# Linear attention and a gated FFN on one core: a table of 3101 steps planned anew

## The chip, the core and the metric

The kernel runs on one core of a Trainium2 chip. The metric is the device time of one execution in microseconds. Four engines compute: TensorE (PE, with its weight loads PEld), VectorE (DVE), ScalarE (ACT) and GpSimd (POOL). SyncE (SP) issues most of the DMAs, POOL the rest. Each engine works through its own list of instructions strictly in order, and waits where an instruction needs something that another engine or a DMA has not delivered yet.

## What is computed

```python
# attention: batch 8, heads 8, sequence 576, head size 64
q_s = exp(q - max(q, axis=-1));  q_s /= sum(q_s, axis=-1) + 1e-9
k_s = exp(k - max(k, axis=2));   k_s /= sum(k_s, axis=2) + 1e-9
kv = einsum('bhsd,bhse->bhde', k_s, v)
x = einsum('bhsd,bhde->bhse', q_s, kv)      # as 4608 tokens x 512
# gated FFN: 512 -> 1536 -> 512
xn = x / sqrt(mean(x * x, axis=-1) + 1e-6) * rms_g
g = xn @ w_gate
out = (g * sigmoid(g) * (xn @ w_val)) @ w_out
```

q, k, v, rms_g are float32; the three weights come in as float64.

## The kernel before

The tokens are worked in nine blocks of 512 (index j, 0 to 8), the hidden size of 1536 in twelve slices of 128 (index i). A matmul in full float32 takes two passes, so most operands are split into a high and a low part that are each exact in a faster format (`_hi` and `_lo` steps), and three products of the parts are added up in PSUM. Blocks 0 to 2 are computed as written: `f1` is one slice of gate or value (twelve matmuls of 128x512), `f2` one slice of the output product. Blocks 3 to 8 go in three pairs p, in which seven products (`pp`, six matmuls each) take the place of eight, with sums on DVE (`c_`), and `f2p` as output product.

Everything is a chain of small steps. A step is one function of the kernel with its indices, as `f1.13.0` (slice 13, that is block 1, slice 1; gate). The order in which the steps are written out is a table of 3101 names, the string `ORDER` at the top of the file. The program takes the names one by one and calls the functions; a letter behind a colon says on which engine a step runs that could run on several (A for ACT, D for DVE, P for POOL). The tile framework adds the waits. So the table sets three things: each engine's list, the engine of many steps, and which buffer of a rotating pool a step gets, with the wait that comes from that buffer's last user.

The steps that matter here:

- `k_load`, `v_load`, `q_load` and `load_w` (from lines 475, 499, 627, 418) are DMAs on SP's queue. A `v_load` of a later batch is five DMAs, a `q_load` four or eight, a `k_load` three.
- `v_ones` (line 514) is a memset on POOL that fills the column of ones beside v, in the same tile into which `v_load` writes.
- For keys, by batch b and pair of heads g: `k_max`, `k_tr` (PE), `k_top`, `k_diag`, `k_rows` (PE), `k_sub`, `k_exp`, then `k_mm` (PE, line 566), which needs v, and `k_eps`, `k_rec`, `kv_norm0`, `kv_hi`, `kv_lo`.
- For queries: `q_max`, `q_sub`, `q_exp`, `q_sum`, `q_rec`, `q_mul`, `q_t`, and `q_x`, the matmul with kv, which gives x. In block 0 they are named with a 0 (`q_sub0`, line 658, and `q_mul0`, line 674, run on POOL). Then `x_sq`, `x_hi`, `x_lo`, `n_sum` and the steps `n_t`, `n_y0`, `n_y1`, `n_rows` for the norm.
- `conv_mul`, `conv_shift`, `conv_sign`, `conv_low`, `conv_add` turn a slice of float64 weights into float32; `w_hi`, `w_lo`, `o_hi`, `o_lo` split it. `s_add`, `s_hi`, `s_lo` prepare the sums of weights that the pairs use.
- `g_mul` (DVE, line 965) reads what `f1.i.0` left in PSUM, `silu` (ACT) and `h_mul` (DVE, line 972) follow. There are two banks of PSUM for gate and value, so `f1.13.0` can start when `g_mul.12` has read its bank.
- `warm` is matmuls without use, which keep PE busy in the first stage.

Of the kernel before, what the change touches and what calls it, by code (L numbers as in the profile page):

```python
# [27 lines left out]
load_w.0.0 k_sub.0.0 v_load.0.3 k_exp.0.2 k_tr.0.1 q_sum0.0.2 warm.9 k_exp.0.0 q_max0.0.0 v_load.0.1 q_eps0.0.2
k_top.0.1 conv_mul.0.1 q_sub0.0.0:P q_rec0.0.2 k_sub.0.3 q_mul0.0.2:P conv_shift.0.1 q_exp.0.0 load_w.1.1
conv_low.0.1.1 q_max0.0.3 warm.2.12 q_t0.0.2 k_diag.0.1:A conv_sign.0.1 q_sub0.0.3:P k_exp.0.3 warm.2.5 g_load  # L30
q_max0.0.1 warm.2.3 load_w.1.0 v_ones.0.3 k_max.1.0 k_mm.0.0 conv_add.0.1.1 q_exp.0.3 q_c0.0.2:A warm.2.11 q_load0.1.0
conv_mul.0.0 k_mm.0.2 k_eps.0.0 q_sub0.0.1:P q_sum0.0.0 conv_low.0.0.1 k_rec.0.0 k_tr.1.0 conv_shift.0.0 warm.2.9
q_exp.0.1 k_rows.0.1 q_eps0.0.0 k_eps.0.2 k_mm.0.3 k_top.1.0 k_rec.0.2 q_rec0.0.0 conv_sign.0.0 kv_norm0.0.2:A
q_mul0.0.0:P k_diag.1.0:A k_sub.0.1 load_w.1.2 kv_norm0.0.0:A conv_add.0.0.1 q_t0.0.0 q_load0.1.1 q_sum0.0.1 k_exp.0.1
k_rows.1.0 q_x0.0.2 k_eps.0.3 q_sum0.0.3 q_c0.0.0:A q_eps0.0.1 k_mm.0.1 k_rec.0.3 w_hi.0.0.2:A q_eps0.0.3 q_rec0.0.1
k_sub.1.0 q_mul0.0.1:P q_x0.0.0 conv_mul.1.1 k_eps.0.1 q_rec0.0.3 k_rec.0.1 q_mul0.0.3:P kv_norm0.0.1:D kv_norm0.0.3:A
warm.2.0 load_w.2.1 conv_shift.1.1 conv_mul.1.0 q_t0.0.1 load_w.2.2 x_hi.0.2:A q_t0.0.3 conv_shift.1.0 load_w.0.2
q_c0.0.1:A conv_sign.1.1 load_w.3.2 x_sq.0.0 q_x0.0.1 x_lo.0.2 q_c0.0.3:A q_max0.1.0 x_sq.0.2 n_sum0.0 k_load.1.1
x_hi.0.0:A conv_sign.1.0 q_sub0.1.0:P q_x0.0.3 x_sq.0.1 q_max0.1.1 x_hi.0.1:A n_sum0.1 x_lo.0.0 q_sub0.1.1:P load_w.2.0
x_sq.0.3 x_lo.0.1 n_sum0.2 q_exp.1.0 w_lo.0.0:P load_w.3.0 x_hi.0.3:A q_sum0.1.0 n_sum0.3 k_exp.1.0 x_lo.0.3 f1.0.0.0.0  # L40
conv_low.1.0.2 v_load.1.0 f1.0.0.0.1 n_t.0 f1.0.0.0.2 f1.0.0.0.3 f1.0.1.0.0 q_eps0.1.0 f1.0.0.1.0 n_y0.0 q_exp.1.1
conv_add.1.0.2 f1.0.1.0.1 f1.0.1.0.2 conv_mul.0.2 f1.0.1.0.3 n_y1.0 f1.0.0.1.1 f1.0.0.1.2 f1.0.0.1.3 f1.0.1.1.0
f1.0.1.1.1 f1.0.1.1.2 f1.0.1.1.3 f1.0.0.2.0 w_lo.0.1:P n_rows.0 w_hi.1.0.2:A f1.0.0.2.1 f1.0.0.2.2 load_w.3.1
f1.0.0.2.3 q_rec0.1.0 f1.0.1.2.0 load_w.5.0 g_mul.0 conv_mul.2.1 f1.0.1.2.1 w_lo.1.0:P f1.0.1.2.2 load_w.5.1 f1.0.1.2.3
conv_shift.0.2 f1.1.0 silu.0 conv_shift.2.1 q_mul0.1.0:P q_load0.1.2 conv_sign.0.2 w_lo.1.1:P conv_low.0.2.1 h_mul.0
conv_mul.2.0 conv_sign.2.1 f1.1.1 conv_low.2.0.2 conv_add.0.2.1 conv_shift.2.0 q_sum0.1.1 conv_low.2.2.1 load_w.4.0
v_ones.1.2 conv_sign.2.0 load_w.4.2 conv_mul.3.0 q_eps0.1.1 q_load0.1.3 conv_mul.1.2 conv_add.2.0.2 conv_shift.3.0 f2.0
conv_low.3.2.1 q_rec0.1.1 conv_sign.3.0 conv_low.1.2.1 conv_shift.1.2 conv_mul.3.1 conv_sign.1.2 q_mul0.1.1:P
w_hi.2.0.2:A g_mul.1 load_w.6.0 conv_shift.3.1 conv_low.3.0.2 load_w.4.1 w_lo.2.0:P k_mm.1.0 conv_sign.3.1 silu.1
f1.2.0 k_eps.1.0 w_lo.2.1:P k_rec.1.0 conv_mul.2.2 q_max0.1.2 kv_norm0.1.0:A h_mul.1 conv_low.5.0.2 conv_add.3.0.2  # L50
conv_shift.2.2 q_t0.1.0 q_max0.1.3 f1.2.1 q_c0.1.0:A conv_sign.2.2 conv_add.1.2.1 load_w.7.0 g_mul.2 conv_mul.4.0
load_w.7.1 silu.2 conv_shift.4.0 k_load.1.2 conv_add.2.2.1 w_hi.3.0.2:A conv_sign.4.0 q_x0.1.0 k_max.1.1 q_sub0.1.3:P
conv_mul.3.2 load_w.5.2 f2.1 x_sq.1.0 load_w.6.1 q_sub0.1.2:P x_hi.1.0:A conv_shift.3.2 q_load.2.0 conv_sign.3.2
w_lo.3.1:P h_mul.2 conv_mul.4.1 x_lo.1.0 conv_low.4.0.2 w_lo.3.0:P conv_shift.4.1 f1.3.1 conv_mul.4.2 conv_sign.4.1
q_exp.1.2 conv_shift.4.2 conv_add.4.0.2 conv_sign.4.2 q_exp.1.3 k_tr.1.1 f1.3.0 k_top.1.1 k_max.1.2 k_diag.1.1:A
conv_add.3.2.1 conv_mul.5.0 load_w.8.1 load_w.8.0 w_hi.4.0.2:A n_cols.0 load_w.6.2 conv_shift.5.0 load_w.7.2
conv_low.5.2.1 w_lo.4.1:P k_rows.1.1 g_mul.3 f2.2 conv_low.4.2.1 conv_sign.5.0 conv_low.7.0.2 conv_add.4.2.1 k_sub.1.1
conv_mul.5.1 q_sum0.1.3 w_lo.4.0:P silu.3 conv_shift.5.1 conv_sign.5.1 v_ones.1.1 v_load.1.1 f1.4.0 load_w.8.2
conv_mul.6.0 conv_add.5.0.2 h_mul.3 conv_low.6.0.2 q_max.2.0 q_sum0.1.2 conv_mul.6.1 f1.4.1 q_eps0.1.2 w_hi.5.0.2:A
load_w.10.0 q_rec0.1.2 q_eps0.1.3 load_w.10.1 conv_shift.6.0 q_mul0.1.2:P k_exp.1.1 conv_shift.6.1 w_lo.5.0:P  # L60
conv_sign.6.1 f2.3 g_mul.4 w_lo.5.1:P conv_mul.5.2 q_half.2.0 o_hi.4:A conv_sign.6.0 silu.4 conv_shift.5.2
conv_add.6.0.2 conv_sign.5.2 conv_mul.7.0 k_mm.1.1 f1.5.0 conv_add.5.2.1 k_eps.1.1 k_load.1.3 k_rec.1.1 q_rec0.1.3
conv_shift.7.0 kv_norm0.1.1:A h_mul.4 kv_hi.1.1:A kv_zero.2 conv_sign.7.0 v_load.1.2 h_hi.4:A o_hi.5:D conv_mul.6.2
q_t0.1.1 h_lo.4:D f1.5.1 q_c0.1.1:A o_lo.5:P conv_shift.6.2 conv_mul.7.1 conv_sign.6.2 conv_low.6.2.1 o_lo.4:P
q_max2.2.0 conv_shift.7.1 w_hi.6.0.2:A conv_sign.7.1 q_x0.1.1 v_ones.1.3 g_mul.5 conv_add.7.0.2 conv_mul.8.2 f2.4
x_sq.1.1 conv_shift.8.2 x_hi.1.1:A conv_sign.8.2 x_lo.1.1 conv_mul.8.0 w_lo.6.0:P load_w.9.1 silu.5 conv_shift.8.0
load_w.9.0 f1.6.0 conv_low.7.2.1 q_load.2.1 h_mul.5 conv_add.6.2.1 conv_mul.7.2 conv_sign.8.0 conv_low.8.2.1
conv_shift.7.2 w_lo.6.1:P h_hi.5:A conv_mul.8.1 conv_sign.7.2 f1.6.1 w_hi.7.0.2:A h_lo.5:D conv_add.7.2.1
conv_shift.8.1 conv_mul.9.1 g_mul.6 kv_hi.1.0:A conv_sign.8.1 q_mul0.1.3:P load_w.9.2 silu.6 conv_shift.9.1 f2.5
conv_mul.9.0 w_lo.7.0:P h_mul.6 conv_low.8.0.2 w_lo.7.1:D o_hi.7:A h_hi.6:A conv_add.8.0.2 conv_shift.9.0 f1.7.0  # L70
conv_low.9.0.2 conv_sign.9.0 conv_sign.9.1 o_hi.6:A o_lo.6:P load_w.11.1 load_w.10.2 k_tr.1.2 f1.7.1 k_top.1.2
load_w.11.0 h_lo.6:P q_max.2.1 k_diag.1.2:A w_hi.8.0.2:A q_half.2.1 conv_add.9.0.2 g_mul.7 conv_mul.9.2 silu.7
conv_shift.9.2 k_rows.1.2 f2.6 conv_low.9.2.1 k_sub.1.2 conv_sign.9.2 h_mul.7 w_lo.8.0:D h_hi.7:A q_t0.1.2
conv_mul.10.1 h_lo.7:P f1.8.0 q_c0.1.2:A conv_shift.10.1 conv_mul.10.2 w_lo.8.1:P conv_sign.10.1 conv_low.10.2.1
conv_shift.10.2 k_exp.1.2 o_lo.7:P conv_sign.10.2 f1.8.1 g_mul.8 x_acc.1.1:P conv_mul.10.0 silu.8 conv_shift.10.0
conv_add.8.2.1 k_max.1.3 k_mm.1.2 f2.7 conv_add.10.2.1 w_hi.9.0.2:A k_eps.1.2 k_rec.1.2 kv_norm0.1.2:D o_hi.8:A
q_sub.2.0:P conv_sign.10.0 conv_low.10.0.2 w_lo.9.0:D q_x0.1.2 h_mul.8 o_lo.8:P kv_hi.1.2:D f1.9.0 h_hi.8:A x_hi.1.2:D
conv_add.10.0.2 x_sq.1.2 x_lo.1.2 q_t0.1.3 g_mul.9 k_tr.1.3 q_c0.1.3:A k_top.1.3 w_lo.9.1:D f1.9.1 silu.9 w_hi.10.0.2:D
k_diag.1.3:A o_hi.10:A h_lo.8:D conv_low.11.0.2 w_lo.10.0:P k_rows.1.3 h_mul.9 f1.10.0 conv_mul.11.0 o_lo.10:P
q_exp.2.0 conv_shift.11.0 conv_sign.11.0 v_ones.2.1 v_load.2.1 v_load.1.3 q_load.2.2 load_w.11.2 k_load.2.0  # L80
conv_add.9.2.1 k_sub.1.3 f2.8 q_sum.2.0 k_exp.1.3 x_acc.1.2:P q_half2.2.0 h_hi.9:A conv_mul.11.1 w_lo.10.1:P q_sum2.2.0
# [1168 lines left out]
```

## Time and profile before

| | |
|---|---|
| median of 3 runs | 961.42 us (960.86 to 962.38) |
| the profiled execution | 962.87 us |
| its span in the profile | 961.1 us |
| PE busy | 943.0 us (98%), 4681 instructions |
| DVE, ACT, POOL busy | 675.4, 448.6, 553.1 us |
| granted TensorE clock, mean | 0.992 |
| read from and written to HBM | 160.49 and 40.89 MB |

The span is the time from the first to the last instruction that the profiler saw; the profiled execution's own time has 1.77 us more around it. A row of a timeline is: start in us, length in us, engine, line, operation, out<-in by the program's names, and in brackets the engine's idle time before it with what ended it. `SPq` is a DMA that SP issues, and its length is the issue alone, not the transfer. PE is at full work where its busy time equals the stretch; matmuls of 512 columns overlap, twelve of them take 2.77 us.

### The profile page before, as it was taken

What the parts mean: (1) busy time and instruction counts of PE and PEld (TensorE: products, weight loads), DVE (VectorE), ACT (ScalarE), POOL (GpSimd) and SP (SyncE); (2) the same over time, 40 slices, a digit from 0 to 9 for tenths busy, and PEclk for the clock granted to TensorE, in tenths of its full rate; (3) what the DMA queues carried; (4) which work ended last, traced back from release to release, by engine and by line L of the source; (5) the groups of instructions that cost most, each with busy time, mean ns of one, the idle gap of its engine ahead of it and who ended that gap; (6) DMA issues with size and microseconds to landing.
All of it is one profiled execution on the core that took longest, in us unless ns stands there. A gap on an engine that the chain in (4) does not pass through costs nothing.

```text
span 961.1 us, 14091 instructions
## 1 busy us (share of the span) xinstructions
PE 943.0 (98%) x4681; PEld 761.5 (79%) x4681; DVE 675.4 (70%) x1420; ACT 448.6 (47%) x714; POOL 553.1 (58%) x570
## 2 busy tenths in 40 slices
...
GB/s 242 284 263 181 104 94 198 300 302 276 307 199 209 184 241 246 180 271 219 202 216 225 160 239 169 222 200 172 203 195 195 260 175 244 179 155 239 143 162 166
DMA packets 164436, 202.32 MB, mean 211 GB/s; under 512 B 105060, under 2 KB 126860, under 8 KB 159756
## 3 DMA queue, kind: packets, MB, share of 16 engines
...
q8 instruction: 37, 0.61, 0.3%
...
HBM read 160.49 MB, written 40.89 MB: 210 GB/s over the span
## 4 chain that ended last, share of the span: by engine, by line
PE 85%; DMA 5%; DVE 4%; POOL 2%; SPq 1%; issue 1%; ACT 1%; DVEq 0%; POOLq 0%
PE ps_gv L1101 17%; PE ps_gv L960 15%; PE ps_o L1101 12%; PE ps_o L1188 10%; PE ps_o L997 8%; PE ps_a L1101 7%; PE ps_a L1188 5%; PE ps_gv L1188 5%; PE ps_a L566 2%; PE ps_a L772 2%; DMA wd<-parts 1%; DMA vt<-in_v_dram 1%; DMA raw<-in_moe_w_gate_dram 1%; DMA qt<-in_q_dram 1%; PE ps_o L772 1%
## 5 line engine op out<-in xcount | busy, mean ns | idle before, releaser
L960 PE MATMUL ps_gv<-xh,w 128*128 128x512 f32 x576 | 191.2, 400 | 2.2 <-DVE rs L584 1.1
L1101 PE MATMUL ps_gv<-x,ring 128*128 128x512 f32 x576 | 141.6, 390 | 0.0
L960 PEld LDWEIGHTS ps_gv<-xh,w 128*128 128x128 f32 x576 | 108.7, 189 | 28.0 <-DVE w L884 1.4
L1101 PEld LDWEIGHTS ps_gv<-x,ring 128*128 128x128 f32 x576 | 107.6, 188 | 22.4
L960 PE MATMUL ps_gv<-xl,w 128*128 128x512 f32 x288 | 112.5, 394 | 0.0
L1122 DVE TENSOR_TENSOR tmp<-tmp,ps_gv 128x512 f32<-128x512 f32 x84 | 57.2, 682 | 63.2 <-PE ps_gv L1101 62.1
L1074 POOL DMA_DIRECT2D ring<-wd x54 | 29.9, 554 | 121.8 <-PE ps_gv L1101 52.9
L1101 PE MATMUL ps_o<-x,ring 128*128 128x512 f32 x360 | 85.0, 390 | 0.6 <-DVE tmp L1122 0.6
L1101 PEld LDWEIGHTS ps_o<-x,ring 128*128 128x128 f32 x360 | 67.5, 188 | 15.1 <-DVE tmp L1122 1.0
L997 PE MATMUL ps_o<-o,hh 128*128 128x512 f32 x256 | 67.5, 406 | 0.0
L960 PEld LDWEIGHTS ps_gv<-xl,w 128*128 128x128 f32 x288 | 54.6, 190 | 11.1 <-issue 0.7
L884 POOL TENSOR_TENSOR w<-w,w 128x512 fp32r<-128x512 f32 x40 | 53.8, 1352 | 12.6 <-ACT w L388 9.7
L1122 DVE TENSOR_TENSOR tmp<-tmp,ps_o 128x512 f32<-128x512 f32 x42 | 28.7, 685 | 40.1 <-PE ps_o L1101 35.7
L997 PEld LDWEIGHTS ps_o<-o,hh 128*128 128x128 f32 x256 | 47.9, 193 | 11.0 <-issue 0.7
L388 ACT CAST hh<-gs 128x512 fp32r<-128x512 f32 x53 | 32.6, 616 | 43.9 <-DVE gs L1138 14.4
L1170 POOL TENSOR_TENSOR hl<-gs,hh 128x512 fp32r<-128x512 f32 x26 | 34.0, 1307 | 23.2 <-DVE hh L388 18.6
L1074 POOL DMA_DIRECT2D w<-wd x18 | 10.2, 564 | 48.8 <-PE ps_a L1101 27.1
L1188 PE MATMUL ps_o<-o,hh 128*128 128x512 f32 x144 | 37.5, 392 | 0.0
L1101 PE MATMUL ps_a<-x,ring 128*128 128x512 f32 x144 | 37.2, 394 | 0.0
L1101 PE MATMUL ps_a<-x,w 128*128 128x512 f32 x144 | 37.2, 394 | 0.0
L519 DVE TENSOR_REDUCE cm<-kt 116x128 f32<-116x640 f32 x28 | 37.0, 1320 | 0.1
L892 POOL TENSOR_TENSOR o<-w,o 128x512 fp32r<-128x512 f32 x21 | 30.3, 1444 | 10.7 <-ACT o L388 5.3
...
## 6 DMA issues: line engine op xcount, KB each, us to landing
...
```

Of the source, the lines that this page charges most:

```text
L388: (e.copy if e is nc.scalar else e.tensor_copy)(dst, src)
L519: nc.vector.tensor_reduce(out=cm, in_=kt_[b, g].rearrange("p h j d -> p h d j"), axis=AX.X, op=ALU.max)
L772: nc.tensor.matmul(px[:, c0:c1], lhsT=wt, rhs=mv[:, c0:c1], start=(i == 0), stop=(i == 2))
L884: on(nc.gpsimd).tensor_tensor(out=w[:, :, 1], in0=halves(s % NF, a, 1)[:, 0], in1=w[:, :, 0].bitcast(F32), op=ALU.subtract)
L892: on(nc.vector).tensor_tensor(out=ol, in0=W(s % NF, 2), in1=oh.bitcast(F32), op=ALU.subtract)
L960: nc.tensor.matmul(pd[s], lhsT=w[:, a, c // 2, m, c % 2 * P:c % 2 * P + P], rhs=X[j, c][x], start=(n == 1), stop=(n == 3 * NKT))
L997: nc.tensor.matmul(po[t], lhsT=a[:, t * P:(t + 1) * P], rhs=w, start=(i == 0 and n == 0), stop=(i == NF - 1 and n == len(terms) - 1))
L1074: nc.gpsimd.dma_start(t, src.rearrange("p a b f -> p (a b f)"))
L1101: nc.tensor.matmul(abc[p, i, m, b], lhsT=src[:, h, c * P:(c + 1) * P], rhs=operand(o, c, x), start=first and n == 0, stop=n == 5, skip_gro ...
L1122: nc.vector.tensor_tensor(out=dst, in0=ux[u + (src,)], in1=abc[u + (b,)], op=ALU.add)
L1170: on(nc.gpsimd).tensor_tensor(out=hl, in0=h_src(p, t, c), in1=HH[p, t, c][0].bitcast(F32), op=ALU.subtract)
L1188: nc.tensor.matmul(pa[p, t, k], lhsT=a[:, k * P:(k + 1) * P], rhs=w, start=(c == 0 and n == 0), stop=(c == NF - 1 and n == 2))
```

## The change

The table `ORDER` is replaced by another with the same 3101 steps. No function of the kernel changes, no step is added or taken out, the sizes and the number of buffers stay. The new table comes from a planner that was run again: like an earlier try that planned all steps anew, it counts with half the clock for PE in the first stage and with loads that are late, and it takes its table from searches with smaller random delays. 294 steps get another engine among ACT, DVE and POOL, in both directions and with little change in the sums (w_lo on POOL 40 before and 45 now, t_add on POOL 9 and 12, hp_lo on POOL 42 and 39, s_lo on POOL 17 and 13). The position of nearly all steps changes. In the first stage the steps `v_ones` of block 0 and its `v_load` move behind other work, which the first lines of the table show:

```diff
 ORDER = """
-exp_table k_load.0.2 k_load.0.3 kv_zero.0 kv_zero.1 k_load.0.0 constants q_load0.0.2 v_ones.0.1 v_ones.0.2 warm.2.2
-kv_zero.4 v_ones.1.0 kv_zero.7 warm.2.8 k_load.0.1 kv_zero.3 warm.2.10 k_max0.0.2 v_ones.0.0 kv_zero.6 load_w.0.1
...
+exp_table k_load.0.0 k_load.0.3 v_ones.1.1 constants q_load0.0.0 v_ones.0.2 kv_zero0.0 warm.2.13 k_load.0.2 warm.2.3
...
```

The new file has one line less ahead of the functions, so that a line of the changed kernel carries a number that is one lower. Three places show what the new table does to the engines' lists.

DVE, about the end of block 0's slices and the start of block 1's: what stands behind `g_mul.11` (gs<-ps_gv,r), before. xl is `x_lo.1.3`, ql `n_lo.1`, kv_lo `kv_lo.1.1`:

```order
L965 TENSOR_TENSOR gs<-ps_gv,r 128x512
L794 SCALAR_TENSOR_TENSOR xl<-ps_a,g_sb,xh 128x512
L808 TENSOR_TENSOR ql<-acc,qh 128x512
L388 CAST o<-w_92 128x512
L972 TENSOR_TENSOR gs<-ps_gv,gs 128x512
L602 TENSOR_TENSOR kv_lo_111<-ot,kv_hi_110 128x128
L884 TENSOR_TENSOR w<-w_92,w 128x2x256
L892 TENSOR_TENSOR o<-w_97,o 128x512
L933 TENSOR_TENSOR sums<-w_92 128x512
L717 TENSOR_TENSOR qt<-qt,sw 128x512
```

DVE in the changed kernel, from the same `g_mul.11`:

```order
L964 TENSOR_TENSOR gs<-ps_gv,r 128x512
L971 TENSOR_TENSOR gs<-ps_gv,gs 128x512
L883 TENSOR_TENSOR w<-w_92,w 128x2x256 x2
L932 TENSOR_TENSOR sums<-w_92 128x512
L716 TENSOR_TENSOR qt<-qt,sw 128x512
L932 TENSOR_TENSOR sums<-w_93 128x512
L826 STREAM_TRANSPOSE sq<-ps_a 128x512
```

`x_lo`, `n_lo`, `o_hi`, `kv_lo` and `o_lo` have left the place between `g_mul.11` and `g_mul.12`, to another engine or another place in the list; the two `w_lo` of slice 12 stand right behind `h_mul.11`.

SP, at the keys and values of batch 5, before: kt is `k_load.5.2`, vt is `v_load.5.1`:

```order
L483 DMA kt<-in_k_dram 112x2x320
L483 DMA kt<-in_k_dram 3x2x320
L484 DMA kt<-in_k_dram 1x10x64
L508 DMA vt<-in_v_dram 112x5x64 x2
L508 DMA vt<-in_v_dram 3x5x64 x2
L510 DMA vt<-in_v_dram 1x2x64
```

SP in the changed kernel, at the same place:

```order
L507 DMA vt<-in_v_dram 112x5x64 x2
L507 DMA vt<-in_v_dram 3x5x64 x2
L509 DMA vt<-in_v_dram 1x2x64
L482 DMA kt<-in_k_dram 112x2x320
L482 DMA kt<-in_k_dram 3x2x320
L483 DMA kt<-in_k_dram 1x10x64
```

The three rows of `v_load.5.1` have moved ahead of the three of `k_load.5.2`. On PE, `k_mm.5.0` has moved ahead of `f2.31`, and between it and `k_mm.5.1` stand f2.31, f1.33, f2.32 and f1.34 now, f1.33, f2.32 and f1.34 before.

POOL, in the first stage, before: w_94 and w_93 are the tiles that `v_ones` writes for pairs 0 and 3, qt and r are `q_sub0`, xl is `q_mul0`:

```order
L515 MEMSET w_94 96x12
L580 MEMSET kv_hi_112 128x128
L580 MEMSET kv_lo_113 128x128
L576 MEMSET ot 128x512 x2
L580 MEMSET kv_hi_110 128x128
L580 MEMSET kv_lo_111 128x128
L658 TENSOR_TENSOR qt<-qt,st 128x512 x2
L674 TENSOR_TENSOR xl<-qt,sm 128x2x4x64
L658 TENSOR_TENSOR r<-r,st 128x512
L515 MEMSET w_93 96x12
```

POOL in the changed kernel, from its first `q_sub0`:

```order
L657 TENSOR_TENSOR qt<-qt,st 128x512
L579 MEMSET kv_hi_108 128x128
L579 MEMSET kv_lo_109 128x128
L657 TENSOR_TENSOR qt<-qt,st 128x512 x2
L657 TENSOR_TENSOR r<-r,st 128x512
L514 MEMSET w_94 96x12
L673 TENSOR_TENSOR xl<-qt,sm 128x2x4x64 x3
L514 MEMSET w_93 96x12
```

The memset for pair 0 has moved behind the four `q_sub0`, the one for pair 3 behind three `q_mul0`. In the table each of them now stands ahead of the `v_load` into its tile, so that the load waits for it; `v_ones.0.3` stood behind its `v_load` before.

594 lines of the change are left out of this document (297 added, 297 removed).

## Prediction

> **What bounds the kernel now.** I read the stretches of the span first (busy time of each engine between chosen times), then the timeline of PE where it stood idle, then the engines it waited for. The columns of the stretches are length, busy time of PE, PEld, DVE, ACT and POOL with instruction counts, granted clock, DMA share and GB/s.
>
> ```profile
> span 961.1 us, 14091 instructions
> ```
> ```profile
> 0.00:42.80 42.80, 35.90 (x205) 24.19 (x205) 32.19 (x84) 27.04 (x48) 23.11 (x45) 0.92 1.05 259
> 42.80:149.30 106.50, 106.50 (x513) 80.32 (x511) 92.78 (x171) 84.80 (x127) 90.00 (x72) 1.00 0.57 160
> 149.30:165.00 15.70, 12.96 (x66) 9.93 (x66) 14.38 (x42) 11.31 (x18) 8.37 (x8) 0.89 0.62 223
> 165.00:368.70 203.70, 202.99 (x1124) 165.14 (x1122) 181.33 (x438) 143.81 (x228) 171.97 (x153) 1.00 0.86 255
> 368.70:377.00 8.30, 5.12 (x34) 4.22 (x34) 4.23 (x14) 1.34 (x2) 6.49 (x7) 0.79 1.12 307
> 377.00:950.00 573.00, 572.42 (x2717) 472.08 (x2716) 349.39 (x674) 178.18 (x289) 251.84 (x287) 1.00 0.68 201
> ```
>
> TensorE is the bound from 42.8 us on. In the last 573 us it is idle for 0.58 us, in 165 to 368.7 for 0.71 us, in 42.8 to 149.3 not at all. The same matmuls stand in both kernels, so in those stretches a new order can lose time and hardly win any. What can be won lies in three places: the first 42.8 us, 149.3 to 165 (2.74 us idle, clock 0.89) and 368.7 to 377 (3.18 us idle, clock 0.79). The two later ones cost their idle time and the clock behind it: 0.11 x 15.7 = 1.7 us and 0.21 x 8.3 = 1.7 us. That is 4.5 and 4.9 us, 9.4 us together.
>
> **First place, 149 to 165 us.** PE's timeline (start, length, what, idle time before it and its releaser):
>
> ```profile
> 149.66 1.43 PE L960 MATMUL ps_gv<-xh,w 128*128 128x512 f32 x5 [0.33 <-DVE w L884]
> ...
> 154.27 0.48 PE L548 MATMUL ps_a<-cm,ones 128*116 128x128 f32 x2 [0.69 <-ACT cm L393]
> ...
> 158.12 0.87 PE L566 MATMUL ps_a<-vt,kt 116*64 116x65 f32 x20 [0.62 <-ACT kt L558]
> ...
> 160.34 0.50 PE L960 MATMUL ps_gv<-xh,w 128*128 128x512 f32 x1 [1.10 <-DVE rs L584]
> ```
>
> Four waits, 0.33 + 0.69 + 0.62 + 1.10 = 2.74 us, all behind DVE in the end. The last is the start of f1.13.0, which takes over the PSUM bank that g_mul.12 on DVE must first have read. DVE's timeline shows g_mul.11 and g_mul.12 (the two L965 rows), and the grouped lines of DVE from 143.9 to 163.5 us show what stood there:
>
> ```profile
> 143.94 0.69 DVE L965 TENSOR_TENSOR gs<-ps_gv,r 128x512 f32<-128x512 f32 x1 [0.89 <-PE ps_gv L960]
> ```
> ```profile
> 159.61 0.68 DVE L965 TENSOR_TENSOR gs<-ps_gv,r 128x512 f32<-128x512 f32 x1
> ```
> ```profile
> L884 DVE TENSOR_TENSOR w<-w,w 128x512 fp32r<-128x512 f32 x4 | 3.0, 746 | 0.0
> L808 DVE TENSOR_TENSOR ql<-acc,qh 128x512 fp32r<-128x512 f32 x1 | 1.6, 1595 | 0.0
> ...
> L602 DVE TENSOR_TENSOR kv_lo<-ot,kv_hi 128x128 fp32r<-128x128 f32 x1 | 1.1, 1070 | 0.0
> ...
> L794 DVE SCALAR_TENSOR_TENSOR xl<-ps_a,g_sb,xh 128x512 fp32r<-128x512 f32 x1 | 0.7, 744 | 0.0
> ```
>
> From one g_mul to the next DVE works for 15.7 us without a pause. PE's round between the two is three groups of twelve matmuls and a k_mm (0.87 us above). The chain of work has such groups as
>
> ```profile
> 85.51 2.77 PE ps_gv L960 x12
> ```
>
> so a round is 3 x 2.77 + 0.87 = 9.2 us. DVE is 15.7 - 9.2 = 6.5 us over it. Of this f1.12.1 and f2.11 cover some 2 x 2.77 = 5.5 us between the point where g_mul.12 could have run and the point where its bank is wanted; what is left, 1.0 us, with the waits that delayed the operations ahead of it, is what PE shows.
>
> The change rewrites DVE's list here (its rows stand in the section on the change). x_lo.1.3, n_lo.1 and kv_lo.1.1 are gone from between the two g_mul, and the two w_lo of step 13 that stood ahead of g_mul.12 as well: 0.74 + 1.60 + 1.07 + 2 x 0.75 = 4.9 us. With 15.7 - 4.9 = 10.8 us DVE is 1.6 us over the round, well inside the 5.5 us of cover. I take the whole 4.5 us as won. Its low end is 0 (the work that left shows up as an equal jam elsewhere).
>
> **Second place, 368.7 us.** The matmul that waits, k_mm.5.1, and the DMA queue of SP ahead of its load (kt is k_load.5.2, vt is v_load.5.1):
>
> ```profile
> 371.90 1.07 PE L566 MATMUL ps_a<-vt,kt 116*64 116x65 f32 x20 [3.18 <-DMA vt<-in_v_dram]
> ```
> ```profile
> 357.15 2.41 SPq L483 DMA_DIRECT2D kt<-in_k_dram  x2
> 359.61 0.64 SPq L484 DMA_DIRECT2D kt<-in_k_dram  x1
> 361.12 2.88 SPq L508 DMA_DIRECT2D vt<-in_v_dram  x4
> 364.05 0.61 SPq L510 DMA_DIRECT2D vt<-in_v_dram  x1
> ```
>
> The load was issued from 361.12 on, and used 10.8 us later. In SP's new list (rows in the section on the change) the vt load stands ahead of the kt load, which takes SP from 357.15 to the next issue at 361.12: up to 4.0 us. The plan also puts k_mm.5.0 ahead of f2.31 instead of behind it, so that one more group of twelve (2.77 us) lies between k_mm.5.0, which frees the buffer, and k_mm.5.1. Against a wait of 3.18 us these are 2.8 to 6.8 us; I take the wait and its half clock as gone, 4.9 us. The low end is 2.8 of 3.18 us won with the clock still halved.
>
> **The head, up to f1.** Here the new order costs time. Before, v_ones.0.0 (a memset on POOL, which fills the ones column of the v tile) ran in the first us and v_load.0.0 was issued at 6.92 us. Rows of POOL, SP, DVE, SP's first issue in the chain, and PE:
>
> ```profile
> 9.88 1.04 POOL L658 TENSOR_TENSOR qt<-qt,st 128x512 f32<-128x512 f32 x1 [5.15 <-DVE st L654]
> ...
> 20.72 1.30 POOL L450 TENSOR_TENSOR w<-w,raw 128x512 int32<-128x512 int32 x1
> ```
> ```profile
> 6.92 1.40 SPq L504 DMA_DIRECT2D w<-in_v_dram  x2
> ```
> ```profile
> 4.06 0.56 DVE L527 TENSOR_TENSOR w<-w 96x384 f32<-96x384 f32 x1 [3.20 <-DMA w<-in_k_dram]
> ```
> ```profile
> 0.74 0.40 SPq L479
> ```
> ```profile
> 27.50 1.00 PE L566 MATMUL ps_o<-w,w 96*64 96x65 f32 x24
> ...
> 36.45 1.71 PE L960 MATMUL ps_gv<-xh,w 128*128 128x512 f32 x5
> ```
> ```profile
> 28.19 0.62 ACT L393 ACTIVATE ot<-ps_o,rs 64x64 f32<-64x64 f32 x2
> 28.84 0.63 ACT L437 ACTIVATE ps_a<-raw 128x512 f32<-128x512 f32 x1
> ```
>
> In POOL's new list (rows in the section on the change) the memsets now stand behind arithmetic, v_load.0.0 waits for the first and v_load.0.3 for the second, and SP's queue stands behind each wait: weights, k and q of block 1 come after them. The first q_sub0 can start about when it did, 9.88 us; four of them (4 x 1.04) and two short memsets give 14.4 us for v_load.0.0 instead of 6.92. An issue of two DMAs takes 1.40 us, and the first load on an empty queue landed 4.06 - 0.74 = 3.3 us after its issue, so v_load.0.0 lands at 18.4 and v_load.0.2, right behind, at 19.8. k_mm.0.2 (1.00, like the k_mm.0.1 row) then ends at 20.8, its sums and reciprocals stand on DVE ahead of q_rec0.0.1, and two q_mul0 (2 x 1.04) put v_load.0.3 at 23.4 and, behind a conv_add (1.30) and short memsets, v_load.0.1 at 25.1. It lands at 25.8 + 3.3 = 29.1, where k_mm.0.1 began at 27.50 before: 1.6 us later. Behind it stand in addition k_mm.0.3 (1.00 on PE, like k_mm.0.1) and, on ACT ahead of q_c0.0.3, a kv_norm0 (0.62) and conv_mul.1.0 (0.63): 2.2 us. So f1 starts 3.8 us later than 36.45, and the work behind it moves with it. The cover that hid the loads, early issue, is gone; that is its price. Bounds: 0 if ACT has these two done while it waits anyway and the load lands in 1.6 us less, and 7.5 us if every us in which the DMA queue stands empty (some 10.5 to 14.4 and 19.8 to 23.4) is lost, since the share in the first 42.8 us is 1.05.
>
> On this clock the Trainium skill, "TensorE: Matmul & The Clock Gate", part 1 on the HAM clock gate, says that the clock halves after an idle window of about 3.4 us and returns after a busy one. It speaks against this change, as PE has nothing to do from about 24.5 to 29 us. The trace agrees that it halves, and already after the shorter waits above (0.89 and 0.79). By that rule the sum would be about 1.7 us longer; it is a rival below.
>
> **Everything else.** Some 290 steps change between ACT, DVE and POOL; one like w_lo takes 0.75 us on DVE (L884 above). They lie beside a PE that is busy 572 of 573 us, and I cost them at nothing. The cover is DVE's spare time, 573 - 349 us in the last stretch; in 165 to 368.7 it is only 22 us of 204, where a jam of 1 us would show as such. The small waits left (0.71 + 0.58 us) I take as many after as before. The tail is the same work.
>
> Sum against the profiled span: 961.1 - 9.4 + 3.8 = 955.5 us. The profiled execution took 962.87 us (1.77 us outside the span), the median of the runs is 961.42; taking the difference over to the median gives 961.4 - 5.6 = 955.8 us.
>
> **Rivals.**
> - *The head at half clock.* PE finds no work from 24.5 to 29 us, and pays for the clock behind it what it paid behind each of the two waits, 1.7 us: 955.8 + 1.7 = 957.5 us. For it: the two clocks above. Against: part of PE's work there waits for ACT anyway.
> - *Another late vt load.* The new plan has other short distances between a v load and its k_mm, 8.6 to 10 us of PE work for six of them (groups of twelve matmuls between the two in the order, at the rows' durations). Before, one with 8.6 us missed by 3.18 us. One miss costs 4.9 us: 960.7 us, which is no change.
> - *The jam moves.* Later on DVE has 13.5 us of work in one round (from g_mul.14 to g_mul.15, its operations in the new order at the mean durations of their kinds before); if it is not covered, the first 4.5 us are not won: 960.3 us, no change.
> - *The weights come late (slower).* SP's queue stands empty for 3.9 + 3.6 us in the head, and longer if POOL is late. The DMA share is 1.05 up to 42.8 us, so this is not made up before f1.1. If the conversions of steps 1 to 4 then wait for weights, PE pays the full 7.5 us and two stretches of half clock (2 x 1.7 us), with the same wait once more for v_load.0.1 at about 2 us: 12.9 - 9.4 = 3.5 us slower, 964.9 us. It decides from a loss of 11.3 us in the head, at which the change is slower by over 0.2%. Against it: DMA share falls to 0.57 in the next stretch, so there is room.
>
> **How the numbers follow.** The forecast has a chance of 0.50, the half-clock head 0.15, another late load 0.15, the moved jam 0.08, late weights 0.10; 0.02 is left for the head at no cost (952.0). A difference under 0.2% (1.9 us) can't be told from none in this kernel: faster 0.67, same 0.23, slower 0.10. The range reaches from the head at no cost, 952.0, past the late load to 962.0.
>
> **What would show it.** Right: no idle time of PE over 0.5 us from 60 to 950 us, clock 1.00 in every stretch behind the head, g_mul.12 within 12 us of g_mul.11, no PE wait for vt, and f1 starting at 40 to 41 us with SP waiting for POOL's memset ahead of v_load.0.0 and v_load.0.3. Wrong: f1 starting before 38 or after 44 us; PE waiting for DVE between 100 and 300 us for over 2 us; a vt wait with a clock below 0.9 behind it.

## The result and the profile after

The changed kernel is slower: 971.21 us (median of 4 runs, 969.62 to 976.19) against 961.90 us of the kernel before, a ratio of 1.011 with a 95% interval of 1.0089 to 1.0131. The profiled execution took 970.76 us, 7.9 us more than that of before; its span is longer by the same 7.9 us. Two of the twelve runs of e16_ktop below (1341.79 and 2414.47 us) and two of the runs of before beside the experiments (1166.95 and 3514.79 us) lie far outside all others and are left out of the medians and ratios. These are the stretches of the prediction, in the changed kernel (the columns are the same):

```profile
span 969.0 us, 14038 instructions
```
```profile
0.00:42.80 42.80, 31.92 (x181) 20.66 (x182) 26.77 (x63) 22.30 (x42) 17.73 (x34) 0.88 0.73 203
42.80:149.30 106.50, 104.00 (x500) 77.66 (x499) 95.23 (x182) 84.18 (x126) 93.37 (x80) 1.00 0.65 180
149.30:165.00 15.70, 15.08 (x68) 12.21 (x67) 10.80 (x30) 8.95 (x13) 10.12 (x11) 1.00 0.42 148
165.00:368.70 203.70, 197.34 (x1108) 158.48 (x1106) 179.29 (x426) 143.32 (x227) 158.09 (x140) 1.00 0.85 257
368.70:377.00 8.30, 8.30 (x40) 6.80 (x39) 7.49 (x26) 5.53 (x10) 8.26 (x8) 1.00 0.63 148
377.00:950.00 573.00, 571.90 (x2728) 470.85 (x2727) 354.61 (x697) 184.01 (x294) 254.57 (x287) 1.00 0.67 201
```

Both old places look mended: 149 to 165 us and 369 to 377 us run at full clock and nearly without idle time. But in the first stretch PE does 4 us less work and the DMA share has fallen from 1.05 to 0.73, and PE is now idle for 2.5 us in 43 to 149 (0 before) and for 6.4 us in 165 to 369 (0.71 before). Since the matmuls have shifted, stretches by time compare different work. The starts of the same matmuls on PE's timeline don't. Each stretch below holds the same matmuls in both kernels.

| stretch of PE | before, us | after, us | difference |
|---|---|---|---|
| start to f1.2.0 | 52.5 | 58.1 | +5.6 |
| f1.2.0 to f1.12.0 | 94.7 | 98.4 | +3.7 |
| f1.12.0 to f1.14.0 (first place) | 24.3 | 19.5 | -4.8 |
| f1.14.0 to f1.24.0 | 95.5 | 96.5 | +1.0 |
| f1.24.0 to f1.33.0 | 87.4 | 93.6 | +6.2 |
| f1.33.0 to the first pp (second place) | 29.2 | 25.5 | -3.7 |
| first pp to the end of the span | 577.5 | 577.4 | -0.1 |

So the two places gave 8.5 us, close to the 9.4 of the prediction. The head took 5.6 us, and 10.9 us went in the stretches between. PE is idle there for 9.3 us, against 0.7 in before; the other 2.3 us stand as longer busy time of the same matmuls at full clock, which is not explained here. The waits of PE by what it waited for (us in total, times, longest), the largest that concern these stretches:

```profile
PE ps_o L565 <- DMA w<-in_v_dram: 6.4, 4, 3.9
PE ps_o L996 <- DVE hh L387: 2.4, 1, 2.4
PE ps_a L821 <- DVE ql L807: 1.9, 1, 1.9
...
PE ps_a L565 <- ACT kt L557: 1.4, 1, 1.4
PE ps_gv L959 <- DVE gs L971: 1.4, 1, 1.4
```

The first row is the head: the v loads. SP's wait for POOL's memsets, SP's issues, the memsets, and PE's waits for the loads and its first f1:

```profile
SPq L503 <- POOL w L514: 12.7, 3, 6.0
```
```profile
13.65 2.74 SPq L503 DMA_DIRECT2D w<-in_v_dram  x4
...
24.88 3.88 SPq L503 DMA_DIRECT2D w<-in_v_dram  x4
```
```profile
22.75 2.04 POOL L673 TENSOR_TENSOR xl<-qt,sm 128x512 f32<-128x512 f32 x2 [6.43 <-DVE sm L669]
24.73 0.12 POOL L514 MEMSET w<- 96x12 f32 x1
...
27.38 0.11 POOL L514 MEMSET w<- 96x12 f32 x1
```
```profile
16.75 0.33 PE L565 MATMUL ps_o<-w,w 96*64 96x65 f32 x2 [3.92 <-DMA w<-in_v_dram]
...
30.31 0.30 PE L565 MATMUL ps_o<-w,w 96*64 96x65 f32 x2 [1.35 <-DMA w<-in_v_dram]
31.06 1.61 PE L565 MATMUL ps_o<-w,w 96*64 96x65 f32 x46 [0.45 <-DMA w<-in_v_dram]
...
41.73 1.25 PE L959 MATMUL ps_gv<-xh,w 128*128 128x512 f32 x3
```

The loads were issued at 13.65 and from 24.88 on, as SP had to stand for 12.7 us behind three of POOL's memsets of 0.12 us; k_mm.0.1 got going at 31.06 (27.50 before), f1 at 41.73 (36.45 before).

The other rows are four single waits. The largest is f2.9 at 144 us. PE, DVE and POOL there; hh is `h_hi.9`, o is `o_lo.9`, kv_hi is `kv_hi.1.2`, POOL's row is a conv_add:

```profile
144.19 2.06 PE L996 MATMUL ps_o<-o,hh 128*128 128x512 f32 x8 [2.36 <-DVE hh L387]
```
```profile
138.68 2.12 DVE L387 CAST kv_hi<-ot 128x128 fp32r<-128x128 f32 x1
140.72 0.68 DVE L964 TENSOR_TENSOR gs<-ps_gv,r 128x512 f32<-128x512 f32 x1
141.32 0.74 DVE L793 SCALAR_TENSOR_TENSOR xl<-ps_a,g_sb,xh 128x512 fp32r<-128x512 f32 x1
141.98 1.73 DVE L891 TENSOR_TENSOR o<-w,o 128x512 fp32r<-128x512 f32 x1
143.63 0.41 DVE L387 CAST hh<-gs 128x512 fp32r<-128x512 f32 x1
```
```profile
138.29 2.42 POOL L449 TENSOR_TENSOR w<-w,raw 128x1024 int32<-128x1024 int32 x1 [3.21 <-ACT xh L392]
```

f2.9 needs `h_hi.9`, `o_lo.9` and `h_lo.9`. Before, they stood on ACT, POOL and POOL; the change put all three on DVE, in one row behind a cast.

### The profile page after: what moved, and what is told of

It is laid out like the page before. It is cut to its first block, busy times and chain, and to the rows that moved or that the text cites. A ratio compares the mean times of both kernels' runs of the same rounds, so it can differ in the third digit from the quotient of the medians.

```text
span 969.0 us, 14038 instructions
## 1 busy us (share of the span) xinstructions
PE 943.5 (97%) x4681; PEld 758.7 (78%) x4681; DVE 679.7 (70%) x1427; ACT 452.1 (47%) x717; POOL 544.6 (56%) x560
## 4 chain that ended last, share of the span: by engine, by line
PE 75%; DMA 8%; DVE 8%; SPq 3%; issue 2%; ACT 2%; POOL 2%; DVEq 0%; POOLq 0%; ACTq 0%
PE ps_gv L1100 17%; PE ps_o L1100 12%; PE ps_o L1187 10%; PE ps_gv L959 9%; PE ps_a L1100 7%; PE ps_a L1187 5%; PE ps_gv L1187 5%; PE ps_o L996 5%; DMA qt<-in_q_dram 3%; DMA vt<-in_v_dram 2%; DMA kt<-in_k_dram 2%; SPq L633 2%; PE ps_a L565 1%; SPq L507 1%; PE ps_gv L454 1%
## 5 line engine op out<-in xcount | busy, mean ns | idle before, releaser
L883 POOL TENSOR_TENSOR w<-w,w 128x512 fp32r<-128x512 f32 x45 | 59.9, 1340 | 15.0 <-ACT w L387 6.7
L518 DVE TENSOR_REDUCE cm<-kt 116x128 f32<-116x640 f32 x28 | 36.9, 1318 | 7.7 <-DMA kt<-in_k_dram 7.7
L1169 POOL TENSOR_TENSOR hl<-gs,hh 128x512 fp32r<-128x512 f32 x22 | 28.8, 1309 | 17.1 <-ACT hh L387 10.5
L1100 PE MATMUL ps_a<-x,w 128*128 128x512 f32 x144 | 36.9, 392 | 0.0
L980 POOL TENSOR_TENSOR hl<-gs,hh 128x512 fp32r<-128x512 f32 x24 | 32.4, 1351 | 6.1 <-ACT hh L387 3.1
L387 ACT CAST w<-w 128x1024 fp32r<-128x1024 f32 x29 | 30.4, 1047 | 10.9 <-DMA wd<-w 7.4
```

What stands on the lines that cost most here:

```text
L387: (e.copy if e is nc.scalar else e.tensor_copy)(dst, src)
L518: nc.vector.tensor_reduce(out=cm, in_=kt_[b, g].rearrange("p h j d -> p h d j"), axis=AX.X, op=ALU.max)
L883: on(nc.gpsimd).tensor_tensor(out=w[:, :, 1], in0=halves(s % NF, a, 1)[:, 0], in1=w[:, :, 0].bitcast(F32), op=ALU.subtract)
L980: on(nc.gpsimd).tensor_tensor(out=hl, in0=g_[s], in1=h_[s][0].bitcast(F32), op=ALU.subtract)
L1100: nc.tensor.matmul(abc[p, i, m, b], lhsT=src[:, h, c * P:(c + 1) * P], rhs=operand(o, c, x), start=first and n == 0, stop=n == 5, skip_gro ...
L1169: on(nc.gpsimd).tensor_tensor(out=hl, in0=h_src(p, t, c), in1=HH[p, t, c][0].bitcast(F32), op=ALU.subtract)
```

## The experiments

Each kernel's list of steps differs from another's by a few listings only, or joins the front of one list with the rest of another (e1, e2, e11, e15). Theory A, at the start: two separate losses, the late head and the new waits behind it. Theory B: the late head alone, the waits behind it being its backlog. The table gives, from each profile, the start of f1, the time from f1.2.0 to f1.24.0 and from there to the first pp, then the median of the runs and the ratio to before's runs of the same session, whose median was 960.9 to 962.7 us.

| kernel | f1 | f1.2 to f1.24 | to pp | median, us | ratio (95%) |
|---|---|---|---|---|---|
| before | 36.45 | 214.5 | 116.6 | 961.42 | |
| after | 41.73 | 214.4 | 119.1 | 971.21 | 1.011 (1.0089 to 1.0131) |
| e1_before_head | 36.0 | 215.0 | 117.4 | 967.94 | 1.0062 (1.0038 to 1.0086) |
| e2_after_head | 44.1 | 214.5 | 116.1 | 970.41 | 1.0092 (1.0073 to 1.0111) |
| e3_two_places | 36.2 | 214.3 | 116.5 | 962.90 | 1.0012 (0.9999 to 1.0025) |
| e4_early_ones | 31.9 | 214.2 | 116.5 | 960.25 | 0.9989 (0.9966 to 1.0011) |
| e5_five_waits | 32.1 | 214.4 | 115.3 | 958.21 | 0.9947 (0.9929 to 0.9965) |
| e6_one_memset | 37.6 | 216.7 | 115.9 | 965.88 | 1.0039 (1.0016 to 1.0061) |
| e7_queue | 38.3 | 213.3 | 115.5 | 961.43 | 1.0003 (0.9980 to 1.0026) |
| e8_warm | 43.1 | 216.3 | 116.9 | 970.08 | 1.0072 (1.0041 to 1.0102) |
| e9_less_work | 31.9 | 215.7 | 114.1 | 957.30 | 0.9943 (0.9924 to 0.9962) |
| e10_before_less | 38.9 | 213.9 | 113.8 | 962.05 | 1.0002 (0.9979 to 1.0025) |
| e11_early_head | 31.6 | 214.5 | 116.3 | 959.24 | 0.9963 (0.9943 to 0.9984) |
| e12_head_queue | 31.9 | 215.7 | 115.6 | 959.69 | 0.9969 (0.9950 to 0.9988) |
| e13_two_more | 32.2 | 212.7 | 115.2 | 957.40 | 0.9960 (0.9945 to 0.9975) |
| e14_queue_qmax | 32.3 | 214.4 | 111.3 | 955.44 | 0.9944 (0.9926 to 0.9963) |
| e15_best | 32.0 | 213.4 | 112.9 | 955.25 | 0.9939 (0.9918 to 0.9960) |
| e16_ktop | 31.2 | 214.0 | 116.9 | 958.21 | 0.9966 (0.9945 to 0.9987) |

A profile is one execution, and the same head does not always take the same time: f1 started at 36.0 to 38.3 us with before's head (before, e1, e3, e7), at 41.7 and 44.1 with after's (after, e2), and at 31.2 to 32.3 with that of e4 (e4, e5, e11 to e16). Differences of 2 us in that column mean nothing. The stretches behind it repeat better. With after's list there (after, e1, e4, e6, e8), the two old places take 43.9 to 45.3 us together (53.5 in before), and the three stretches between the head, the two places and pp 286.2 to 288.5 us (277.6 in before).

### The head and the rest apart

e1 joins before's list up to f1.5.0 with the rest of after's; e2 is the other way round. The join of e1, against before:

```diff
 k_mm.1.1
-f1.5.0 conv_add.5.2.1 k_eps.1.1 k_load.1.3 k_rec.1.1
+kv_hi.1.0:A kv_lo.1.0:P v_ones.1.3 q_load.2.1 o_lo.4:P q_rec0.1.3
...
```

> The list of before up to f1.5.0, and behind it what is left of the list of after, in its order and on its engines. Theory A (two separate losses: the head starts PE's steady work 5.6 us late, and the lists behind it have a dozen short waits of PE, 10.6 us in place of 7.2, which use up what the two old places gave): the head's loss is gone and the waits behind it stay, so 971.2 - 5.6 = 965.6 us, 0.3 to 0.5 % slower than before. Theory B (the order behind the head is sound and its short waits are only the late head's backlog on DVE, POOL and the load queue): with an early head they go, and the 9.4 us of the two old places are won: about 952.5 us.

> The counterpart: the list of after up to f1.5.0, and behind it the list of before. Theory A: before plus the head's 5.6 us, with the old waits at 160 and 370 us in place: 967.5 us. Theory B: the late head makes backlog behind it in this list too, so 969 to 972 us, with new waits of PE between 100 and 400 us besides the two old ones.

Measured 967.94 and 970.41 us. e1 starts f1 at 36.0 us and is still slower than before, with f2.9 waiting 1.8 us and k_mm.4.3 1.4: theory B is out. e2 is by its time in B's range, but not by its trace: f1 began at 44.1, and from f1.2.0 to the end of the span it took as long as before (908.1 against 908.6 us), with the two old waits and one of 1.05 us where the lists join. The lost time is the head's own.

### What makes the head late

e4 takes after's list and puts the three memsets at the start; e6 moves one of them alone.

```diff
 q_load0.0.0 v_ones.0.2
+v_ones.0.1 v_ones.0.3 v_ones.0.0
...
-v_ones.0.0
 v_load.0.0 v_load.0.2
...
-v_ones.0.3
 v_load.0.3
...
-v_ones.0.1
 v_load.0.1
```

> After with one edit: v_ones.0.0, v_ones.0.3 and v_ones.0.1 listed at the start beside v_ones.0.2, so that POOL fills the ones columns in the first microseconds and the v loads of block 0 wait for nothing on POOL. Theory A1 (the head is late because SP's queue stands behind these memsets): v_load.0.0 is issued before 9 us, f1 starts at 37 to 38 us, and 4 us come back: 967 us. Theory A2 (the head is late for its own order of loads and its steps on ACT and DVE, weights of step 1 among them, whatever the memsets do): f1 stays at 41 to 42 us and the time at 970 to 971 us.

> After with v_ones.0.0 alone listed at the start; v_ones.0.3 and v_ones.0.1 stay behind the q_mul0 as in after. If the first memset does the harm (it holds SP's queue until 13.65 us and everything behind it): f1 at 33 to 35 us, 962 to 964 us. If the two later ones do (the last v load ends the head): f1 at 40 to 41 us, 969 to 970 us. If each does its share: f1 at 36 to 38 us, 965 to 967 us.

e4 gave 960.25 us, 11 us less than after and 7 us less than I had expected. SP's issues, PE's f1 and the first stretch of e4:

```profile
8.14 2.76 SPq L503 DMA_DIRECT2D w<-in_v_dram  x4
14.02 3.85 SPq L503 DMA_DIRECT2D w<-in_v_dram  x4
```
```profile
31.86 1.26 PE L959 MATMUL ps_gv<-xh,w 128*128 128x512 f32 x3
```
```profile
0.00:42.80 42.80, 36.48 (x223) 24.62 (x224) 35.93 (x89) 31.09 (x55) 25.88 (x43) 1.00 1.05 271
```

The loads go out 5.5 and 10.9 us earlier, the DMA share is 1.05 again and the clock full, and f1 starts 9.9 us earlier than in after, even 4.6 us earlier than in before. So the new head is the better one but for three memsets that take 0.12 us each. In e6 (f1 at 37.6, 965.88 us) PE waits once more for the last v load:

```profile
25.20 0.45 PE L565 MATMUL ps_o<-w,w 96*64 96x65 f32 x2 [4.25 <-DMA w<-in_v_dram]
```

The first memset is worth 4.1 us of f1's start, the two later ones 5.7 us, each figure with the spread of 2 us above: each does its share.

e8 fills PE's wait ahead of k_mm.0.0 in after with dummy matmuls, to see whether the half clock is what is paid.

```diff
 warm.9
+warm.2.11 warm.2.2 warm.2.10 warm.2.6 warm.2.7 warm.2.12
```

> After with six of the dummy warm matmul steps moved from later in the head to right behind warm.9, where PE stands idle for 3.9 us ahead of k_mm.0.0 and the clock is half from 16.9 to 27.1 us. If the half clock is what makes the head late: clock full to 27 us, f1 2 to 3 us earlier (39 us), 968 to 969 us. If the late loads do, and PE at half clock would have waited for them anyway: f1 at 41 to 42 us, 970 to 971 us, whatever the clock shows.

Measured 970.08 us, f1 at 43.1. The wait shrank from 3.92 to 0.23 us, but half clock came all the same, from 19.8 to 26.6 and 30.1 to 36.9 us, as PE then ran out of work further on. Time and f1 fit the late loads; the clock's part is not separated by this run.

### The two places, one by one

e3 mends the two places in before by three listings.

```diff
+v_load.5.1
 k_load.5.2
...
-v_load.5.1
...
-kv_lo.1.1:D
+kv_lo.1.1:P
...
+g_mul.12
 k_rows.2.0
```

> Before with four edits at the two old places alone: v_load.5.1 listed ahead of k_load.5.2, kv_lo.1.1 on POOL in place of DVE, g_mul.12 listed ahead of k_rows.2.0 and so ahead of two w_lo and an s_add on DVE. The prediction's price for the two places, 4.5 + 4.9 us, says 961.9 - 9.4 = 952.5 us, no half clock behind the head and no PE wait over 0.5 us at 150 to 165 and at 369 us. The rival (such a wait only moves to the next place, since DVE and the queue stay as full): 959 to 962 us with new waits of PE near by.

962.90 us, nothing won. The waits are where the rival said; PE at both places, and DVE at the second:

```profile
154.08 0.47 PE L548 MATMUL ps_a<-cm,ones 128*116 128x128 f32 x2 [0.92 <-ACT cm L393]
158.74 0.87 PE L566 MATMUL ps_a<-vt,kt 116*64 116x65 f32 x20 [1.44 <-ACT kt L558]
...
372.14 0.43 PE L534 MATMUL ps_a<-ident,cm 116*128 116x116 f32 x1 [3.30 <-DVE cm L519]
```
```profile
370.76 1.23 DVE L519 TENSOR_REDUCE cm<-kt 116x128 f32<-116x640 f32 x1 [5.89 <-DMA kt<-in_k_dram]
```

k_mm.5.1 got its vt in time; k_tr.5.2 waited 3.30 us in its stead, since k_load.5.2 had been pushed back. e7 pushes a q load back instead, and e12 is the same behind e4's head. e11 is that head (e4's list up to f1.5.0) with before's list behind it.

```diff
-q_load.6.2
...
 v_ones.5.1
+v_load.5.1 k_load.5.2 q_load.6.2
...
-q_max.6.2
...
+q_max.6.2
 q_half.6.2
```

> Before with SP's list alone changed around 350 us (and one DVE step that would wait for it): v_load.5.1 right behind v_ones.5.1, then k_load.5.2, then q_load.6.2, which stood ahead of both; q_max.6.2 moved to its q_half.6.2. The prediction's price for the second place (3.18 us of wait and 1.7 us of half clock, won by an earlier v load): 961.9 - 4.9 = 957 us, no PE wait over 0.5 us from 350 to 400 us. Rival R (the load queue is full there and the wait passes on to the load that was pushed back, as k_tr.5.2 did in e3_two_places): 960 to 963 us, a wait of 2 us or more within 30 us of the old one.

> The list of e4_early_ones (after with the three memsets early) up to f1.5.0, and the list of before behind it. If head and rest add up: f1 at 32 us in place of 36.45, and all of it kept, 962.0 - 4.6 = 957.4 us. Rival (what the head wins is lost again behind it, since loads and conversions of the next steps are no earlier): 960 to 962 us, with PE waits between 40 and 150 us, where before has none.

> e11_early_head with the four listings of e7_queue around 350 us (v_load.5.1, k_load.5.2, q_load.6.2, q_max.6.2). If the queue edits are worth what the profile of e7_queue shows up to the first pp (2 us): 955.5 us. If they only pass the wait on, as the time of e7_queue says: 957 to 958 us, the same as e11_early_head.

961.43, 959.24 and 959.69 us. e11 shows that the early head adds up with before's list, somewhat short of what was expected (957.4). e7 and e12 win nothing: the wait has moved on once more. DVE and PE in e12, where the first row is `q_max.6.2` (it reads qt, whose load was issued from 358.49 us on; the row names another load that landed with it) and gs is `g_mul.34`:

```profile
369.23 0.69 DVE L700 TENSOR_REDUCE st<-qt 128x16 f32<-128x512 f32 x1 [4.52 <-DMA vt<-in_v_dram]
...
370.67 0.69 DVE L965 TENSOR_TENSOR gs<-ps_gv,r 128x512 f32<-128x512 f32 x1
```
```profile
371.41 0.50 PE L960 MATMUL ps_gv<-xh,w 128*128 128x512 f32 x1 [2.10 <-DVE gs L965]
```

PE's releaser is g_mul.34, but that only stood in line behind `q_max.6.2`, which stood for 4.52 us in front of a late q load. e14 takes it out of the line.

```diff
 h_mul.34
+q_max.6.2 q_half.6.2 q_max2.6.2
```

> e12_head_queue with one thing more: q_max.6.2 and the two steps that need it listed behind h_mul.34 on DVE. In e12_head_queue DVE stood for 4.5 us in front of q_max.6.2, whose q load I had moved back, with g_mul.34 behind it and f1.35.0 waiting for that (2.10 us and half clock). Theory H (the second place is a wait at the head of an in-order list, and goes when nothing on the path stands behind a late load): no PE wait over 0.5 us from 340 to 400 us, pp starts 327 to 328 us after f1.2.0 (331 in before and in e12), 956 us. Rival R (the load queue is full there, so some load is always late by 2 us): the wait turns up at a third place, 959 to 960 us.

955.44 us: PE has no wait of 0.1 us or more between 340 and 400 us, and f1.24.0 to pp takes 111.3 us (116.6 in before). The second place does yield, once nothing that PE needs stands behind a late load.

### Why the waits between came back

e5 is e4 with five short waits mended.

```diff
-kv_hi.1.2:D
+kv_hi.1.2:A
...
+w_hi.12.0.2:A
 w_hi.13.0.2:A
...
+h_mul.20
 q_half.3.3
...
+h_lo.24:P
 s_lo.5.4:P
...
+k_rows.4.3 k_sub.4.3
 q_max.5.1
```

> After with the three memsets early (as in e4_early_ones, 960.3 us) and six listings changed, one or two for each of five short waits of PE: kv_hi.1.2 on ACT in place of DVE (ahead of h_hi.9 and so f2.9, 2.23 us), w_hi.12 ahead of w_hi.13 on ACT (f1.12.0, 0.62), h_mul.20 ahead of q_half.3.3 on DVE (f1.21.1, 0.60), h_lo.24 ahead of s_lo.5.4 on POOL (f2.24, 0.87 + 0.25), k_rows.4.3 and k_sub.4.3 ahead of q_max.5.1 (k_mm.4.3, 1.15). Theory A (each wait is a producer that the list puts too close to its consumer, and goes with that listing): 5.7 us of waits and 1.7 us of half clock behind f2.9 come back, 952.9 us, none of the five left over 0.3 us. Rival R (a repaired wait only moves to the next place, as in e3_two_places): 958 to 961 us, with as much PE idle time from 60 to 400 us as in e4_early_ones.

958.21 us, in the rival's range, and PE waits as long from 60 to 400 us as in e4. f2.9 and k_mm.4.3 no longer wait, and f1.12.0 comes 94.5 us after f1.2.0 (99.3 in e4). But twelve slices on nothing is left of these 4.8 us: f1.24.0 is 214.4 us after f1.2.0 (214.2 in e4), for other waits have appeared, the longest of them

```profile
151.36 0.48 PE L547 MATMUL ps_a<-cm,ones 128*116 128x128 f32 x2 [1.72 <-ACT cm L392]
```

at the first place. Then it had to be asked whether DVE and POOL are too full there. e9 (e5's list) and e10 (before's) do not compute the low parts q_lo, x_lo and h_lo and take the high parts in their place, so that their results are not the right ones; h_lo as an example:

```diff
-        hl = fp.tile([P, TB], F32R, name="hl", bufs=2)
-        on(nc.gpsimd).tensor_tensor(out=hl, in0=g_[s], in1=h_[s][0].bitcast(F32), op=ALU.subtract)
-        h_[s].append(hl)
+        h_[s].append(h_[s][0])
```

> The list of e5_five_waits with work left out: the low parts of q, x and h (q_lo, x_lo, h_lo) are not computed, and the high part stands in for them in the matmuls, so PE has the same matmuls to do while DVE has some 18 us and POOL some 41 us less between 60 and 380 us. None of the waits of PE that e5_five_waits has there (7.0 us in all) is on one of these three. Theory L (DVE and POOL are so full there that a wait which is taken away forms again at the next place): the waits shrink to under 3 us although the list is the same, about 954 us. Theory A (each wait is one badly placed listing): k_rows.2.0 (1.7), k_tr.3.1 (1.2), k_rows.3.2, f2.24 and the others stay, 957 to 959 us.

> Before with the same work left out (q_lo, x_lo and h_lo not computed, the high part standing in for them), list unchanged. Theory L: the jam at 150 to 165 us (2.74 us of waits and 1.7 us of half clock) goes, the wait for vt at 372 us stays since it is a load's: 962.0 - 4.5 = 957.5 us. Theory A: the jam is an order of DVE's list, of which only x_lo.1.3 (0.74 us) is among the work left out: 961 to 962 us.

957.30 and 962.05 us: with a twentieth less work on DVE from 60 to 380 us (268 us in place of 282 in e9) and a sixth less on POOL the waits stay, in e9 one of them longer than in e5:

```profile
153.90 0.78 PE L547 MATMUL ps_a<-cm,ones 128*116 128x128 f32 x2 [3.04 <-ACT cm L392]
```

So it is not the load over the whole stretch. e13 and e16 follow that wait up DVE's and ACT's lists; e15 puts e16's list up to f1.24.0 and e14's behind it together. (The wait for v at k_mm.5.1, expected to stay in e10, was 2.34 us there and left the clock full.)

```diff
-w_hi.13.0.2:A
...
 silu.11
+w_hi.13.0.2:A
...
+store.1.3:A
 s_hi.5.4:A
```
```diff
+k_top.2.0
 s_add.0.1:D
...
+k_diag.2.0:A
 s_hi.0.1:A
```

> The list of e5_five_waits (958.2 us) with two more listings changed on ACT: w_hi.13 behind silu.11, and store.1.3 ahead of s_hi.5.4. In e9_less_work ACT stood for 3.6 us in front of w_hi.13, which waits for the matmuls of f1.11.1 to free its buffer, and silu.11, h_mul.11 and w_lo.12 stood behind it. Theory H (the waits that came back are steps stuck behind a step that itself waits, on an engine that takes its list in order; they can be had one by one): f1.12.0 (0.67), k_rows.2.0 (1.72) and most of f2.24 (0.91) go and nothing else appears, about 955 us, and f1.24.0 comes 2 us earlier after f1.2.0 than the 214.4 us of e5_five_waits. Rival R (something else sets the pace up to f1.24.0, which lies 214.2 to 215.0 us behind f1.2.0 in before, after, e1, e2, e3, e4 and e5 alike): still 214 us or more, 957 to 959 us.

> The list of e13_two_more (957.4 us) with k_top.2.0 listed ahead of s_add.0.1 on DVE, and k_diag.2.0 ahead of s_hi.0.1 on ACT: in e13_two_more PE waits 3.2 us for k_rows.2.0 at 152 us, and k_top.2.0 stood on DVE behind s_add.0.1, q_sub.2.1, s_add.1.1, n_t.1 and n_y0.1 from 147 us on, though k_tr.2.0 was done at 144 us. Theory H: that wait and its half clock go, f1.24.0 lies 208 to 210 us behind f1.2.0, 952 to 953 us. Rival R (DVE's work in that round is too much whatever its order): the wait comes back as one for another DVE step between 150 and 165 us, 956 to 958 us.

> The list of e16_ktop up to f1.24.0 and that of e14_queue_qmax behind it: the early head, the first stretch of after with its repairs, the second place of before with its repair. Theory H: 212.7 - 3.2 - 1.7 = 207.8 us from f1.2.0 to f1.24.0, then 111.3 us to pp as in e14_queue_qmax, 955.4 - 6.6 = 949 us. Rival R: the stretch up to f1.24.0 takes 212 us or more again, 954 to 956 us.

957.40, 958.21 and 955.25 us. In e13 f1.12.0 no longer waits and 1.7 us come back up to f1.24.0, but k_rows.2.0 waits 3.23 us. In e16 that wait is gone, and two others stand in its place. PE, and the stretch around it:

```profile
153.10 0.32 PE L533 MATMUL ps_a<-ident,cm 116*128 116x116 f32 x1 [1.58 <-DVE y L844]
154.69 0.87 PE L565 MATMUL ps_a<-vt,kt 116*64 116x65 f32 x20 [1.27 <-ACT kt L557]
```
```profile
142.60:159.50 16.90, 13.90 (x72) 10.86 (x71) 16.34 (x38) 11.04 (x17) 12.63 (x12) 0.90 0.48 177
```

DVE is busy for 16.34 of 16.90 us there. This is the jam of before again, and no order that was tried gets past it: f1.14.0 lies 116.9 to 120.5 us behind f1.2.0 in before, after and all the runs. How many steps DVE has in this round does not settle it. From g_mul.11 up to g_mul.12 they are the same 25 in after and nine of the runs, but their lengths add up to 10.3 to 10.4 us in after, e1, e4, e6 and e8, and to 11.7 to 13.8 us in e5, e9, e13, e15 and e16. Two of these steps, `q_sub.2.1` and `s_add.1.1`, and POOL beside them, first in e4, then in e13:

```profile
149.32 0.69 DVE L716 TENSOR_TENSOR qt<-qt,sw 128x512 f32<-128x512 f32 x1
149.92 0.69 DVE L932 TENSOR_TENSOR sums<-w 128x512 f32<-128x512 f32 x1
```
```profile
150.66 1.30 POOL L980 TENSOR_TENSOR hl<-gs,hh 128x512 fp32r<-128x512 f32 x1 [4.03 <-DVE sums L932]
```
```profile
146.52 1.77 DVE L716 TENSOR_TENSOR qt<-qt,sw 128x512 f32<-128x512 f32 x1
148.22 1.76 DVE L932 TENSOR_TENSOR sums<-w 128x512 f32<-128x512 f32 x1
```
```profile
146.01 1.74 POOL L883 TENSOR_TENSOR w<-w,w 128x512 fp32r<-128x512 f32 x1
147.85 1.58 POOL L980 TENSOR_TENSOR hl<-gs,hh 128x512 fp32r<-128x512 f32 x1
```

In e4 POOL stands idle beside them. In e13 it works, and the two DVE steps take 1.8 us in place of 0.7. POOL's first row in e13 is `w_lo.13.0`, which needs `w_hi.13` from ACT; e5 put w_hi.12 ahead of w_hi.13, and e13 moved w_hi.13 back once more, so that POOL's work came to lie beside DVE's. This is read off the rows. A list that takes the waits away and keeps POOL clear of these steps wasn't tried, so whether the jam can be passed stays open. e15 and e14 have the lowest medians and beat both kernels; between the two no difference can be told, and their intervals overlap that of e5.

## Why the prediction was wrong

**The head** (predicted +3.8, measured +5.3 us at f1 and 5.6 at f1.2.0). The mechanism was right and its steps came close: v_load.0.0 issued at 13.65 (14.4 predicted), v_load.0.3 at 24.88 (23.4), k_mm.0.1 at 30.3 to 31.1 (29.1). The term was too small by 1.5 us, which is no more than one execution differs from the next; the second and third `q_mul0` came later, as POOL stood idle for 6.43 us ahead of them, waiting for DVE. PE's long wait was not from 24.5 to 29 us, as the prediction had it, but the 3.92 us up to 16.75. The clock was half for 10.2 us from 16.9 us on, against 6.8 us in before's head, so the rival of the half clock came true at least in part; what it cost is not separated (e8). What the prediction did not see is what the memsets cost in the new head: 10 us (e4), half of it hidden because the rest of that head is 4.6 us faster than before's.

**First place** ("I take the whole 4.5 us as won"). In its own stretch 4.8 us were won, but 3.7 us had gone just ahead of it, 2.36 of them at f2.9. The prediction's count of DVE's work held: its steps between g_mul.11 and g_mul.12 add up to 10.4 us, where 10.8 were predicted. When e5 took the waits at f2.9 and at the start of f1.12.0 away, the jam was back. e5 changes two things here, though: PE comes earlier, and `w_lo.13` on POOL comes later, beside DVE's steps; which of the two brought the jam back is not separated. Counting up to f1.14.0, after has won 1.1 us over before (117.9 against 119.0), not 4.5. The rival of the moved jam comes nearest to this, but it looked for the jam behind the place and not ahead of it, and had a chance of 0.08.

**Second place** (predicted 4.9, measured 3.7 us in its stretch). The wait for vt is gone. e3, e7 and e12 show that the swap on SP, one of the two things on which the prediction rested, is not enough for it in before: whichever load is pushed back makes the next step late. What the other, the earlier k_mm.5.0, does alone wasn't tried. The stretch ahead, f1.24.0 to f1.33.0, is 6.2 us longer in after. One of its waits is n_sum.4 at 359.31 us, 1.89 us long, on `n_lo.4`, which the change moved from POOL to DVE:

```profile
357.03 0.69 DVE L699 TENSOR_REDUCE st<-qt 128x16 f32<-128x512 f32 x1 [3.63 <-DMA qt<-in_q_dram]
...
358.57 0.68 DVE L807 TENSOR_TENSOR ql<-acc,qh 128x512 fp32r<-128x512 f32 x1
```

On DVE it stands behind a q_max that stood for 3.63 us in front of a late q load. Whether the load is late differs between executions: with the same list there, n_sum.4 does not wait in e4 and e6, and the stretch takes 91.0 to 93.1 us in e1, e4, e6 and e8 (87.4 in before, 93.6 in after).

**Everything else** ("I cost them at nothing", "the small waits left I take as many after as before"). This is the step that failed: the stretches outside the head and the two places lost 10.9 us. The two longest waits there, f2.9 and n_sum.4, are on steps that the change put on DVE. DVE's spare time was no cover, because part of it lies in front of late loads (3.63 us in the row above) and not where PE waits. Nor is 0.75 us, the row from which the prediction priced such a step, what one takes: `o_lo.9` took 1.73 us on DVE. With 2.36 us at f2.9, one of the prediction's own signs of being wrong came, a wait of PE for DVE of over 2 us between 100 and 300 us. What each of the other waits there comes from was not followed up one by one. The sum by what was measured is -8.5 + 5.6 + 10.9 - 0.1 = +7.9 us. The range ended at 962.0 because each rival was priced against a won 9.4 us; that several happen together, as here, was not among them. Even the rival that came out slower, at 964.9, lay outside the range.
